# A two-stage kernel on one Trainium2 core: expert 0's last three blocks by seven half-size products, and a new instruction order for the first stage

## The chip, the cores and the metric

The program runs on one core of one Trainium2 chip. The metric is the device time of one execution in microseconds (us). Before the change three runs took 753.22, 753.16 and 752.12 us; the median is 753.16.

A core has five engines with queues of their own, each of which works in order: TensorE (PE; matmuls, with PEld for its weight loads), VectorE (DVE), ScalarE (ACT), GpSimd (POOL) and SyncE (SP). Matmul results land in PSUM, eight banks of 128 partitions x 2 KB; SBUF is the working memory. Transfers are issued by an engine's queue and run on 16 DMA engines.

## What is computed

Cross attention between tokens `x` and a small state, in both directions, makes a matrix of 4352 rows (8 batches of 512 + 32 rows) by 512 columns. It goes through a mixture of 8 experts, with routing weights from a Sinkhorn normalisation of 8 rounds.

```python
def _attn_ref(x, state):                      # x 8,8,512,64; state 8,8,32,64
    scores = scale * np.matmul(x, state.transpose(0, 1, 3, 2))
    a = np.exp(scores - scores.max(-1, keepdims=True))
    a /= a.sum(-1, keepdims=True) + 1e-09
    xread = np.matmul(a, state)
    scores2 = scale * np.matmul(state, x.transpose(0, 1, 3, 2))
    a2 = np.exp(scores2 - scores2.max(-1, keepdims=True))
    a2 /= a2.sum(-1, keepdims=True) + 1e-09
    sread = np.matmul(a2, x)
    return np.concatenate([xread, sread], axis=2)

def _moe_ref(x, w_gate, w1, w2):              # x 4352,512; w1 8,512,1024; w2 8,1024,512
    logits = x @ w_gate
    P = np.exp(logits - logits.max())
    for _ in range(8):
        P /= P.sum(1, keepdims=True) + 1e-09
        P /= P.sum(0, keepdims=True) + 1e-09
        P *= N / E
    for e in range(E):
        h = np.maximum(x @ w1[e], 0.0)
        out += P[:, e:e + 1] * (h @ w2[e])
    return out
```

## The kernel before

**Blocks.** The rows are cut into nine blocks: blocks 0 to 7 are the 512 tokens of a batch, block 8 holds the 256 state rows of all batches. Matmul operands are fp16, sums fp32. For blocks 0 to 7 the token rows are never formed: `aT` holds the attention weights, and the first layer uses V = state x w1 (L863 on: projections of 64x32 tiles, two halves `f` for each block), so a tile of 128 hidden units by 512 tokens is two matmuls (L897, L255). Block 8 uses `xsT` and four matmuls of 256 columns.

**Two parts.** The first part (to about 136 us) does attention, the whole of expert 0, Sinkhorn, and the first hidden block of expert 1. It is written as a list of operations `ops`, each with the engines that may do it, its predecessors and its buffers. `PLAN` (L18 to L50) is an order table: each step is the number of an operation and the letter of the engine. `issue` (L105) emits the operations in that order, so it sets the order of every engine's queue. The second part is the loop at L1042 over experts 1 to 7 and their blocks: the second layer of one block is interleaved with the first layer of the next.

**Attention.** Each batch has two units q of four heads; there are 16 units. For a unit: scores in PSUM (L605; the ring "pair" has one slot of two banks); side A transposes by VectorE (L628), maximum (L631), subtraction subA (L648, VectorE), exp (ScalarE), sum and reciprocal (L666, L667), normA (L670, VectorE or GpSimd), transpose back into `aT` (L674). Units 0 and 1 go another way: scores token by token (L684), maxT, subT (L691), and TensorE transposes (turnA L709). Side B takes the maximum (L640), exp (L652), a reciprocal (L659), normB (L662, on GpSimd in 12 units as a tensor_scalar), a transposing transfer on SP's queue (L742), and the matmuls of `read` (L758) that make `xsT`. GpSimd's queue issues the loads of `x_nat` (L468, four buffers) and of weights; SP's queue issues the transposing transfers of `x_nat` to `xT` (L591) from batch 2 on, in one line with those of L742.

**Expert 0.** For each block the hidden tiles go through PSUM to `hT` with a ReLU (L425 on ScalarE or L427 on VectorE). The second layer is dense: for each 128 tokens eight matmuls of 512 columns (L935), then one copy to `acc` (L419 or L421). After Sinkhorn `weigh` (L292) scales the rows of `acc` by expert 0's routing weight.

**Sinkhorn.** Part K: a maximum over the logits (L815), then eight rounds of `rownorm` (five VectorE instructions L829 to L833), a matmul with a matrix of ones (L846), and `colnorm` (three VectorE instructions). The routing weights `Pmat` are needed by the first accumulation of expert 1.

**Experts 1 to 7.** The second layer uses a form of 2x2 block multiplication with seven products in place of eight (`layer2`, L320): the 2x2 quarters are of tokens and hidden units on one side and of hidden units and output columns on the other. Sums of quarters of w2 are in `T` (L204, L965), sums of quarters of the hidden block in `sm` (L281 to L284). A product is eight matmuls of 256 columns into bank A, E or one of two banks B (`seeds`). A product's bank is added to `acc` with the routing weight (L348). Before expert 1's first products two matmuls with the identity (`seed`, L351) write the banks B once.

**End.** The last block's second layer writes its 256 rows in four transfers for each 128 rows, on two queues (L316 to L318).

Of the kernel before, what the change touches and what calls it, by code (L numbers as in the profile page):

```python
# [17 lines left out]
46V 62P 50H 51G 61A 71V 63P 60A 52G 64V 11G 72V 73A 80P 65V 12G 435P 401P 66A 81V 13H 79P 14G 82V 436A 88V  # L18
437A 404P 83A 67V 402A 137H 403A 89V 96H 97P 100P 84V 406A 68V 90A 98A 15G 85V 69P 86P 53G 405A 99V 87V 70A
103P 101A 102A 91V 409P 16H 92G 413P 104V 407P 410A 411P 105V 111A 438P 120P 414V 408A 419P 421P 106V 415P  # L20
112V 138S 121V 74V 439A 412A 422V 113V 417P 107A 54G 440A 75G 122V 432P 429P 123V 370V 420A 469P 128A 418A
416A 17G 108V 140P 124A 125V 423P 426P 471A 433P 114A 148V 93S 129V 430P 149V 172H 424P 76S 434A 115V 470A
109G 130V 139S 110V 126G 141V 131A 427P 18G 127V 142V 428V 431A 445P 143V 132V 94P 150A 95V 77P 425A 156P 116G
447P 151V 133V 78V 449P 446A 443P 441P 144A 455P 164V 152G 448A 117S 19H 450V 157V 444A 165V 173S 442A 451P
456A 166A 134S 20G 452A 453P 463P 158V 472P 207H 145V 175P 159V 183V 184V 457P 31G 146G 454A 176V 473A 160A
464P 185A 174S 460P 458P 461P 465A 147V 161V 21G 153S 177V 191P 47P 162G 474A 118P 167V 459A 154P 462A 178V
163V 135P 49A 168G 199V 22H 48V 179A 466P 136A 352P 475P 200V 192V 201A 193V 119V 467P 476A 194V 23G 195A 485P
202V 208S 210P 180V 169S 155A 218V 356P 353A 481P 357V 468A 487P 219V 24G 489P 181G 186V 211V 242H 486A 482A
477P 490V 488A 483P 479P 220A 170P 478A 503P 187G 480A 484V 171A 203G 196V 537P 209S 25H 212V 226P 197G 504A
505A 506P 213V 500P 182V 198V 26G 234V 221V 507A 222V 204S 188S 491P 27G 538A 227V 539A 501P 497P 502A 508A  # L30
492P 235V 243S 228V 244S 214A 229V 511P 215V 236A 523P 230A 498P 494P 216G 245P 495P 515P 512V 499A 277H 231V
524A 493A 517P 246V 253V 223S 496A 247V 521P 516A 237V 254V 519P 509P 522V 518A 248V 513P 232G 189P 520A 255A
205P 510V 224P 514V 540P 28H 278S 261P 249A 190V 269V 29G 225A 270V 262V 531P 534P 206V 238G 250V 532P 256V
358P 271A 535P 217V 541A 533A 233V 542A 312H 279S 263V 272V 536A 354P 280P 528P 543P 529P 525P 288V 289V 251G
555P 264V 281V 265A 282V 239S 257V 526P 359A 266V 544A 530V 556A 545P 355A 547P 549P 273G 553P 527A 546V 571P
313S 290A 548A 283V 605P 550A 554V 296P 267G 606V 304V 572A 305V 240P 573A 557P 284A 607A 558A 551P 297V 552A
568P 360P 258S 241V 285V 30G 291V 306A 559P 562P 574P 298V 252V 315P 299V 286V 569P 576A 268V 323V 563P 575A
274S 300A 560P 570A 292G 316V 361A 561A 581P 564A 307V 565P 362P 324V 317V 301V 325A 302G 566P 363V 582A 326V
579P 587P 583P 287V 314S 588V 591P 567A 580A 639P 608P 584A 592A 347H 303V 331P 577P 348G 641V 640A 610A 609A
339V 293S 589P 585P 275P 332V 259P 578A 327G 586A 260A 590A 294P 340V 308G 333V 341A 593P 309S 318V 319A 334V  # L40
295V 364P 594P 276V 328S 625P 619P 342V 595A 335A 365A 599P 320V 602P 343V 336V 600P 337V 603P 626A 321G 322V
329P 310P 350G 344S 601A 349G 311A 620V 345P 338V 346V 604V 366P 596P 330A 368P 369V 351G 597P 367A 371V 611P
372P 598A 695H 615P 617P 373V 612V 374P 375V 613P 614V 616A 623P 618A 621P 696H 711H 376A 705P 377V 642P 624A
622A 706A 707A 630P 643V 697V 708P 644A 378P 379V 631P 710A 627P 698V 380V 647P 632A 709A 636P 628P 381P 633P
699V 648V 637P 382V 634P 657P 629A 638A 383V 700V 653P 658A 655P 384P 651P 635A 701V 654A 725P 385V 723P 386V
702V 656A 726A 716P 652A 724A 717A 645P 659P 649P 714P 646A 650A 660A 387P 721P 715A 712P 727P 687P 722A 388V
728A 688A 667P 713A 664P 389V 390P 703V 665P 668P 391V 673P 674A 392V 661P 670P 669A 729V 393P 671P 394V 666A
662P 672A 677P 395V 718P 663A 678A 679P 675P 683P 719A 681P 720V 680A 676A 685P 396P 684A 682A 397V 686A 692P
704V 689P 693P 690P 730P 398V 694A 399P 733P 731V 691A 732A 735A 734A 400V
""".split()  # L50
ENGINES = {"P": "PE", "V": "DVE", "A": "ACT", "G": "POOL", "D": "DMA", "S": "SPQ", "H": "HOST"}
NT_ = 2
ETX = 0
POOLB = 1
X_PACE = 4.4
# [49 lines left out]
def issue(ops):  # L105
    for step in PLAN:
        op = ops[int(step[:-1])]
        assert all(d.end for d in op.after) and ENGINES[step[-1]] in op.on
        for slot in op.takes:
            slot.ring.taken.append(slot)  # L110
            slot.tile = slot.make()
        op.emit(ENGINES[step[-1]])
        op.end = True
    assert all(op.end for op in ops) and len(PLAN) == len(ops)
# [3 lines left out]
def kernel(  # L118
# [63 lines left out]
    outs = out.rearrange("(b s) d -> b s d", s=SB)[:, S:, :]  # L182
# [80 lines left out]
    def layer1(e, bi):  # L263
# [6 lines left out]
        for j in range(NJ):  # L270
            for i in range(2):
                fb = i * NJ + j
                hps = bank([128, S], FP32, "hps", "h")
# [25 lines left out]
    def layer2_last():  # L299
# [4 lines left out]
        nb = 128 // Ns  # L304
        for row in range(tn // 128):
# [10 lines left out]
            for i in range(nb):  # L316
                (nc.scalar if i % 2 else nc.sync).dma_start(
                    out=outs[row * nb + i], in_=acc[ds(i * Ns, Ns), k, :])  # L318

    def layer2(e, bi, n):  # L320
# [30 lines left out]
        def seed(i):  # L351
            bb = bank([128, 2, DH], FP32, "Bseed", "B%d" % i)
            nc.tensor.matmul(bb.rearrange("p c d -> p (c d)"), identh, aT[:, 0, 0], start=True, stop=True)
            seeds.append(bb)

        if not n:
            for k, eng in enumerate(("DVE", "ACT", "DVE", "POOL")):
                weigh(k, eng)
        product(A, h(0, 0), w2h[:, :NJ, :DH], True)
        if not n:  # L360
            seed(0)
        Bb = seeds[n % 2]
        nc.scalar.copy(out=Bb[:, :nk], in_=A[:, :nk])  # L363
        yield
        product(Eb, s(0), T[:, 0], True)
        if not n:
            seed(1)
# [199 lines left out]
    for b in range(B):  # L567
# [30 lines left out]
        for q in range(NQ):  # L598
# [62 lines left out]
            def normB(eng, E2=E2, rrec=rrec):  # L661
                engines[eng].tensor_scalar(out=E2.tile, in0=E2.tile, scalar1=rrec.tile, scalar2=None,  # L662
                                           op0=ALU.mult)
# [33 lines left out]
            else:  # L697
                m0 = op(r(2), {"DVE": (0.63, 0.72)}, flip, [o2], [eA], [ps])
                m1 = op(r(3), {"DVE": (0.59, 0.68)}, maxA, [m0], [mxA], [eA])
                s1 = op(r(4), {"DVE": (0.60, 0.80)}, subA, [m1], [], [eA, mxA])  # L700
# [22 lines left out]
            n2 = op(r(3), {"DVE": (0.10, 0.25)}, biasB, [m2], [nsB], [nmB])  # L723
# [5 lines left out]
            f2 = op(r(6), {"DVE": (0.16, 0.26)}, recB, [e2], [rrec], [rowsum])  # L729
            f2 = op(r(6), {"DVE": (0.35, 0.48), "POOL": (1.56, 1.70)} if POOLB else {"DVE": (0.35, 0.48)}, normB, [f2], [], [E2, rrec])  # L730

# [32 lines left out]
            def keepS(eng, b=b, q=q, su=su):  # L764
                copy(eng, xsT[:, ds(2 * q, 2), ds(b * Ns, Ns)], su.tile)
# [38 lines left out]
    def sk(on, emit, after, **how):  # L804
        return op(rank, on, lambda _: emit(), after, **how)
# [6 lines left out]
    op((30.0,), {"DVE": (0.2, 0.3)}, lambda _: nc.vector.memset(ones128, 1.0))  # L812
# [8 lines left out]
    c = sk({"PE": (0.18, 0.45)}, lambda: nc.tensor.matmul(gb.tile, ones128[0:1, :], sm_["gm"]), [c], takes=[gb])  # L821
# [4 lines left out]
    for it in range(8):  # L826
        def rownorm():
            rsum = tile_of("rsum", [128, NTB])
            nc.vector.reduce_sum(out=rsum, in_=Pmat, axis=AX_X)  # L829
            nc.vector.tensor_scalar(out=rsum, in0=rsum, scalar1=EPS, scalar2=None, op0=ALU.add)  # L830
            nc.vector.reciprocal(out=rsum, in_=rsum)
            nc.vector.tensor_mul(Pmat, Pmat, rsum.unsqueeze(2).broadcast_to((128, NTB, E)))
            nc.vector.reduce_sum(out=tile_of("cpart", [128, E]), in_=Pmat.transpose([0, 2, 1]), axis=AX_X)  # L833

        csb = psum([128, E], FP32, "csb_ps")

        def colnorm(csb=csb):
            crec = tile_of("crec", [128, E])
            nc.vector.tensor_scalar(out=crec, in0=csb.tile, scalar1=EPS, scalar2=None, op0=ALU.add)
            nc.vector.reciprocal(out=crec, in_=crec)  # L840
            nc.vector.scalar_tensor_tensor(out=Pmat, in0=crec.unsqueeze(1).broadcast_to((128, NTB, E)),
                                           scalar=float(N) / float(E), in1=Pmat,
                                           op0=ALU.mult, op1=ALU.mult)

        c = sk({"DVE": (2.10, 2.25)}, rownorm, [c])
        c = sk({"PE": (0.25, 0.60)}, lambda csb=csb: nc.tensor.matmul(csb.tile, ones128, sm_["cpart"]),  # L846
               [c], takes=[csb])
        c = sk({"DVE": (0.75, 0.90)}, colnorm, [c], uses=[csb])
# [193 lines left out]
    for i, (e, bi) in enumerate(work):  # L1042
# [11 lines left out]
        if i:  # L1054
            next(v, None)
# [54 lines left out]
```

## Time and profile before

| what | us |
|---|---|
| median of three runs | 753.16 |
| the profiled execution | 752.75 |
| its span, from first to last instruction | 751.0 |
| first matmul (waits for x_nat) | 6.86 |
| first reduction of Sinkhorn | 100.13 |
| last VectorE instruction of Sinkhorn ends | 136.09 |
| first product of expert 1 | 135.14 |
| last product ends, about | 747.0 |

Times within the profile are counted from the start of the span. Busy time of GpSimd is 70.8 us in all; 22272 packets with 20.97 MB are on its queue. The page's issues of transfers give the time from issue to landing:

```profile
w1h<-in_moe_w_dram POOLq DMA_DIRECT2D x16, 512.0 KB, 7.0
...
x_nat<-in_x_dram POOLq DMA_DIRECT2D x16, 256.0 KB, 5.6
...
xT<-x_nat SPq DMA_TRANSPOSE x12, 4.2
```

The columns are queue, kind, count, size and the median time to landing. An x_nat load is some six microseconds under way from GpSimd's queue, and its transposed copy four more from SP's.

A timeline line reads: start, duration, engine, line, operation, output and input tiles with their shapes, count, and in brackets how long the engine had been idle and what ended it. Neighbouring instructions of one engine overlap by some 0.07 us in the records.

### The profile page before, as it was taken

What the parts mean: (1) busy time and instruction counts of PE and PEld (TensorE: products, weight loads), DVE (VectorE), ACT (ScalarE), POOL (GpSimd) and SP (SyncE); (2) the same over time, 40 slices, a digit from 0 to 9 for tenths busy, and PEclk for the clock granted to TensorE, in tenths of its full rate; (3) what the DMA queues carried; (4) which work ended last, traced back from release to release, by engine and by line L of the source; (5) the groups of instructions that cost most, each with busy time, mean ns of one, the idle gap of its engine ahead of it and who ended that gap; (6) DMA issues with size and microseconds to landing.
All of it is one profiled execution on the core that took longest, in us unless ns stands there. A gap on an engine that the chain in (4) does not pass through costs nothing.

```text
span 751.0 us, 16151 instructions
## 1 busy us (share of the span) xinstructions
PE 736.0 (98%) x6517; PEld 502.2 (67%) x6517; DVE 617.0 (82%) x1529; ACT 517.7 (69%) x1014; POOL 70.8 (9%) x81
## 2 busy tenths in 40 slices
PE   5999999999999999999999999999999999999997
PEld 3444445666777777776776767776777767767776
DVE  5899989877888789788888788887897888887885
ACT  6876856799876766667666766667666676667662
POOL 4674410200010000100000000100001000000000
PEclk9899999999999999999999999999999999999999
DMA  9997560600033000700007000330007000002234
GB/s 179 140 134 131 82 99 1 109 6 1 1 61 53 2 1 2 113 1 2 1 2 112 2 1 1 58 57 1 1 2 112 2 1 2 1 31 94 103 113 141
DMA packets 51323, 36.71 MB, mean 49 GB/s; under 512 B 25392, under 2 KB 43824, under 8 KB 51248
## 3 DMA queue, kind: packets, MB, share of 16 engines
q0 software_dynamic: 22272, 20.97, 18.5%
q1 hardware_dynamic: 27744, 14.18, 7.6%
q8 instruction: 51, 0.84, 0.5%
q10 hardware_dynamic: 1232, 0.52, 0.3%
q14 instruction: 24, 0.20, 0.1%
HBM read 42.48 MB, written 8.91 MB: 68 GB/s over the span
## 4 chain that ended last, share of the span: by engine, by line
PE 92%; DVE 3%; DMA 1%; ACT 1%; POOL 1%; issue 0%; SPq 0%; POOLq 0%; DVEq 0%; ACTq 0%
PE hps L255 28%; PE Bseed L334 20%; PE A L334 14%; PE E L334 14%; PE yps L935 6%; PE hps L897 4%; PE v_ps L235 4%; DMA xT<-x_nat 1%; DMA x_nat<-in_x_dram 1%; PE y L312 0%; PE v_ps L870 0%; POOL a L670 0%; ACT Hm L275 0%; DVE acc L348 0%; POOL E L662 0%; PE su_ps L758 0%
## 5 line engine op out<-in xcount | busy, mean ns | idle before, releaser
L275 ACT ACTIVATE Hm<-hps 128x512 f16<-128x512 f32 (+1 forms) x496 | 265.8, 577 | 130.5 <-PE hps L255 128.1
L255 PE MATMUL hps<-aT,V 128*128 128x512 f16 x880 | 230.6, 379 | 0.0
L334 PEld LDWEIGHTS <-Hm 128*128 128x128 f16 x1888 | 181.6, 98 | 71.3 <-issue 15.9
L348 DVE SCALAR_TENSOR_TENSOR acc<-Bseed,Pmat,acc 128x256 f32<-128x256 f32 x354 | 155.0, 477 | 9.8 <-PE Bseed L334 6.9
L334 PEld LDWEIGHTS <-sm 128*128 128x128 f16 x1416 | 138.3, 98 | 34.5 <-issue 0.3
L334 PE MATMUL A<-w2h,Hm 128*128 128x256 f16 x944 | 123.7, 273 | 0.0
L334 PE MATMUL Bseed<-T,Hm 128*128 128x256 f16 x944 | 123.3, 273 | 0.0
L255 PEld LDWEIGHTS <-V 128*128 128x128 f16 x880 | 86.1, 98 | 50.8
L348 DVE SCALAR_TENSOR_TENSOR acc<-E,Pmat,acc 128x256 f32<-128x256 f32 x236 | 103.2, 476 | 13.8 <-PE E L334 13.5
L281 DVE TENSOR_TENSOR sm<-Hm 128x512 f16<-128x512 f16 (+1 forms) x122 | 50.1, 411 | 60.4 <-ACT Hm L275 60.2
L243 ACT CAST V<-v_ps 128x512 f16<-128x512 f32 x144 | 74.2, 612 | 0.0
L348 DVE SCALAR_TENSOR_TENSOR acc<-A,Pmat,acc 128x256 f32<-128x256 f32 x118 | 51.9, 479 | 17.9 <-PE A L334 17.6
L935 PE MATMUL yps<-w2h,hT 128*128 128x512 f16 x272 | 64.1, 379 | 0.1
L334 PE MATMUL E<-w2h,sm 128*128 128x256 f16 x472 | 61.7, 273 | 0.0
L334 PE MATMUL E<-T,sm 128*128 128x256 f16 x472 | 61.6, 273 | 0.0
L334 PE MATMUL Bseed<-T,sm 128*128 128x256 f16 x472 | 61.5, 272 | 0.0
L363 ACT COPY Bseed<-A 128x512 f32<-128x512 f32 (+1 forms) x62 | 34.1, 550 | 37.9 <-PE A L334 35.3
L282 DVE TENSOR_TENSOR Hm<-Hm 128x512 f16<-128x512 f16 (+1 forms) x122 | 50.3, 412 | 4.2
L284 DVE TENSOR_TENSOR sm<-Hm,sm 128x512 f16<-128x512 f16 (+1 forms) x122 | 50.2, 412 | 4.2
L283 DVE TENSOR_TENSOR sm<-sm,Hm 128x512 f16<-128x512 f16 (+1 forms) x122 | 49.4, 405 | 0.0
L194 POOL DMA_DIRECT2D w1h<-in_moe_w_dram x12 | 8.5, 714 | 396.9 <-PE hps L255 396.5
L935 PEld LDWEIGHTS <-hT 128*128 128x128 f16 x272 | 25.4, 99 | 28.9 <-issue 1.8
(127 smaller groups left out, 617.7 us busy)
## 6 DMA issues: line engine op xcount, KB each, us to landing
w1h<-in_moe_w_dram POOLq DMA_DIRECT2D x16, 512.0 KB, 7.0
w2h<-in_moe_w_dram POOLq DMA_DIRECT2D x16, 512.0 KB, 8.4
out_dram<-acc SPq DMA_DIRECT2D x32, 256.0 KB, 2.5
x_nat<-in_x_dram POOLq DMA_DIRECT2D x16, 256.0 KB, 5.6
st_st<-in_state_dram ACTq DMA_DIRECT2D x1, 256.0 KB, 4.9
st_st<-in_state_dram SPq DMA_DIRECT2D x1, 256.0 KB, 4.2
ETs<-E SPq DMA_TRANSPOSE x16, 4.3
out_dram<-acc SPq DMA_DIRECT2D x4, 64.0 KB, 1.8
```

What stands on the lines that cost most here:

```text
L235: nc.tensor.matmul(ps[q][ds(j * Ns, Ns), :], stT[ds(r, 64), bi, q, ds((j ^ q) * Ns, Ns)], w1h[ds(r, 64), 2 * q + j // 2, cols], tile_posit ...
L243: nc.scalar.copy(out=dst, in_=src)
L255: nc.tensor.matmul(out, lhs, rhs, start=(k == 0), stop=(k == len(terms) - 1))
L275: nc.scalar.activation(out=Hm[:, i, j, :tn], in_=hps[:, :tn], func=AF.Relu)
L281: nc.vector.tensor_add(s1, a21, a22)
L282: nc.vector.tensor_sub(a21, a11, a21)
L283: nc.vector.tensor_sub(s2, s1, a11)
L284: nc.vector.tensor_sub(s4, a12, s2)
L334: nc.tensor.matmul(dst[:, c], lhs(j, c), rhs[:, j], start=first and c == 0 and j == 0, stop=(j == NJ - 1), skip_group_check=True)
L348: nc.vector.scalar_tensor_tensor(out=dst, in0=src[:, c], scalar=p[:, k], in1=dst, op0=ALU.mult, op1=ALU.add)
L363: nc.scalar.copy(out=Bb[:, :nk], in_=A[:, :nk])
L935: nc.tensor.matmul(yps.tile, hT[fb].tile[:, ds(tk * 128, 128)], w2h[:, fb, :], start=(fb == 0), stop=(fb == NFB - 1))
```

## The change

It does six things. (1) Expert 0's blocks 6, 7 and 8 use seven products in the second layer: `strassen_ops` takes the place of the dense form, with sums of w2's quarters made by `sums_w_ops(0)` and of the hidden block's by `sums_h_ops`, each of which may stand on VectorE or GpSimd. The products are not weighted, so they are copied or added to `acc`. (2) The order table is new, and names more operations (833 in place of 736): the five and three VectorE instructions of a Sinkhorn round are operations of their own, so that others can stand between them. (3) A table `IDLE` puts dummy matmuls of 128 columns ahead of five operations. (4) normB on GpSimd is a product with a broadcast column in place of a tensor_scalar, and subA may stand on GpSimd. (5) The two seed matmuls go: the first hidden tile of block (1, 1) is computed in the first bank B, which writes it; the scalings of rows before expert 1's first adds are ordered anew. (6) The state rows are laid out so that 128 rows leave in one transfer for each group of columns.

The planner's cost figures beside the operations changed too; they are not used when the program is built.

```diff
 PLAN = """
 6G 0S 1S 2V 7H 44V 3A 33V 32A 34A 8G 56P 36P 35V 55H 37V 10H 45V 57A 42P 58V 9G 38P 40P 43A 59P 4S 39A 41V 5V
...
+IDLE = {56: 50, 63: 3, 80: 3, 462: 8, 69: 22}
+SB0 = (6, 7, 8)
...
+        idle(op.takes[0].tile if op.takes else None, IDLE.get(int(step[:-1]), 0))
         op.emit(ENGINES[step[-1]])
...
-    outs = out.rearrange("(b s) d -> b s d", s=SB)[:, S:, :]
+    nb = 128 // Ns
+    outs = out.rearrange("(g b s) d -> g s b d", b=nb, s=SB)[:, S:, :, :]
...
-                hps = bank([128, S], FP32, "hps", "h")
+                if lent is None:
+                    hps = bank([128, S], FP32, "hps", "h")
+                else:
+                    hps, lent = lent, None
...
-            for i in range(nb):
-                (nc.scalar if i % 2 else nc.sync).dma_start(
-                    out=outs[row * nb + i], in_=acc[ds(i * Ns, Ns), k, :])
+                (nc.scalar if c + 1 < parts else nc.sync).dma_start(
+                    out=outs[row, :, :, cols], in_=acc[:, k, cols])
...
-        def seed(i):
-            bb = bank([128, 2, DH], FP32, "Bseed", "B%d" % i)
-            nc.tensor.matmul(bb.rearrange("p c d -> p (c d)"), identh, aT[:, 0, 0], start=True, stop=True)
-            seeds.append(bb)
-
         if not n:
-            for k, eng in enumerate(("DVE", "ACT", "DVE", "POOL")):
+            for k, eng in ((2, "DVE"), (3, "POOL"), (0, "DVE")):
                 weigh(k, eng)
         product(A, h(0, 0), w2h[:, :NJ, :DH], True)
+        Bb = seeds[n % 2]
         if not n:
-            seed(0)
-        Bb = seeds[n % 2]
+            yield
         nc.scalar.copy(out=Bb[:, :nk], in_=A[:, :nk])
+        if not n:
+            weigh(1, "ACT")
...
-                engines[eng].tensor_scalar(out=E2.tile, in0=E2.tile, scalar1=rrec.tile, scalar2=None,
-                                           op0=ALU.mult)
+                if eng == "POOL":
+                    nc.gpsimd.tensor_mul(E2.tile, E2.tile, rrec.tile.broadcast_to((128, S)))
+                else:
+                    nc.vector.tensor_scalar(out=E2.tile, in0=E2.tile, scalar1=rrec.tile, scalar2=None, op0=ALU.mult)
...
-                s1 = op(r(4), {"DVE": (0.60, 0.80)}, subA, [m1], [], [eA, mxA])
+                s1 = op(r(4), {"DVE": (0.60, 0.80), "POOL": (1.05, 1.20)}, subA, [m1], [], [eA, mxA])
...
-                copy(eng, xsT[:, ds(2 * q, 2), ds(b * Ns, Ns)], su.tile)
+                copy(eng, xsT.rearrange("p c (g n b) -> p c g n b", g=B // nb, b=nb)[:, ds(2 * q, 2), b // nb, :, b % nb], su.tile)
...
+    def sums_w_ops(e):
...
+        for g in range(2):
+            tg = []
+            for i in range(4):
+                def sub(eng, i=i, g=g):
+                    p, q = quarters(e, tsum[e])[i]
+                    jj = ds(g * (NJ // 2), NJ // 2)
+                    engines[eng].tensor_sub(tsum[e][:, i, jj], p[:, jj], q[:, jj])
...
+    def sums_h_ops(bi, rank, kept, Hm, sm, goal=None):
...
+            def t1(eng, parts=parts):
+                a11, a21, a12, a22, (s1, s2, s4) = parts()
+                engines[eng].tensor_add(s1, a21, a22)
...
+            on = {"DVE": (0.15 + 0.29 * f, 0.25 + 0.29 * f), "POOL": (0.1 + 0.95 * f, 0.25 + 0.95 * f)}
...
+    def strassen_ops(bi, deps, held, Tr):
...
+            def seed(_):
+                nc.tensor.matmul(pair.tile[:, 0], identh, aT[:, 0, 0], start=True, stop=True, skip_group_check=True)
...
+        p1 = product(A, h(0, 0), lambda: w2(0, 0), True, a11 + [ready], [Ab])
+        c1 = op(rank, {"ACT": (0.50, 0.66), "DVE": (0.62, 0.74)}, lambda eng: copy(eng, Bb()[:, :nk], A()[:, :nk]),
+                [p1] + st_last, [], [pair, Ab])
+        p2 = product(Eb, s(0), lambda: T(0), True, s1 + Tr[0] + [ready] + st_last)
+        e11 = put(Eb, 1, 1, [p2])
+        p3 = product(Bb, s(1), lambda: T(1), False, s2 + Tr[1] + [c1])
+        e01 = put(Bb, 0, 1, [p3])
+        p4 = product(A, h(1, 0), lambda: w2(1, 0), False, a12 + [c1])
+        put(A, 0, 0, [p4])
+        p5 = product(Bb, h(0, 1), lambda: T(2), False, s3 + Tr[2] + [e01])
+        x11 = put(Bb, 1, 1, [p5, e11], True)
+        p6 = product(Eb, s(2), lambda: w2(1, 1), False, s4 + [e11])
+        x01 = put(Eb, 0, 1, [p6, e01], True)
+        p7 = product(Bb, h(1, 1), lambda: T(3), False, a12 + s3 + Tr[3] + [x11])
+        y = put(Bb, 1, 0, [p7])
...
+        if bi in SB0:
+            h_ready = strassen_ops(bi, deps, held, Tr0)
+            continue
...
+    def idle(t, n):
...
+        for _ in range(n):
+            if t.dtype == FP16:
+                nc.tensor.transpose(t, identh, identh)
+            else:
+                nc.tensor.matmul(t, identh, identh, start=True, stop=True, skip_group_check=True)
...
+        if not i:
+            seeds += [bank([128, 2, DH], FP32, "Bseed", "B%d" % k) for k in range(2)]
         l2 = layer2(e, bi, i)
-        l1 = layer1(*work[i + 1]) if i + 1 < len(work) and work[i + 1] not in hid else iter(())
+        l1 = iter(())
+        if i + 1 < len(work) and work[i + 1] not in hid:
+            l1 = layer1(*work[i + 1], None if i else seeds[0].rearrange("p c d -> p (c d)"))
+        if not i:
+            next(l2)
+            next(l1)
```

In the new order GpSimd does 12 normB, 12 normA, 12 subA, 7 of the 16 half-sums of w2 (5 for expert 0, 2 for expert 1) and 13 sums of quarters of H; VectorE keeps 2 subA, does 8 of the 80 ReLUs (it did 16) and 9 half-sums of w2. Sinkhorn's first reduction stands behind 42 hidden groups and 40 dense half-groups of TensorE's order, where it stood behind 50 and 48.

## Prediction

> **What bounds the kernel now.** I read the page first: busy shares and the chain that ended last.
>
> ```profile
> PE 736.0 (98%) x6517; PEld 502.2 (67%) x6517; DVE 617.0 (82%) x1529; ACT 517.7 (69%) x1014; POOL 70.8 (9%) x81
> ...
> PE 92%; DVE 3%; DMA 1%; ACT 1%; POOL 1%; issue 0%; SPq 0%; POOLq 0%; DVEq 0%; ACTq 0%
> ```
>
> TensorE carries the chain. The change, however, is almost wholly in the first 136 us (attention, expert 0, Sinkhorn), so next come three windows of that stage. The columns are span, then busy us (and count) of PE, weight loads, DVE, ACT, POOL, then granted clock, DMA share, GB/s.
>
> ```profile
> 0.00:23.00 23.00, 14.00 (x145) 8.20 (x146) 14.12 (x32) 14.46 (x28) 9.84 (x17) 0.85 1.18 179
> 23.00:100.00 77.00, 75.47 (x866) 35.95 (x859) 71.02 (x160) 58.99 (x134) 41.57 (x39) 1.00 0.81 117
> 100.00:136.00 36.00, 35.73 (x227) 18.27 (x225) 31.93 (x89) 22.62 (x47) 0.00 (x0) 1.00 0.20 34
> ```
>
> To 23 us TensorE is little used and its clock is not all granted (0.85). From 23 to 100 us VectorE is at 92% beside a full-looking TensorE; from 100 us GpSimd is empty. Matmuls are pipelined, so "busy" hides small waits; the timeline of TensorE shows them.
>
> ```profile
> 18.86 3.57 PE L897 MATMUL hps<-aT,V 128*128 128x512 f16 x8
> ...
> 22.98 1.90 PE L897 MATMUL hps<-aT,V 128*128 128x512 f16 x8
> ...
> 52.82 0.30 PE L605 MATMUL psB<-xT,stT 64*32 64x256 f16 x8 [0.90 <-DMA xT<-x_nat]
> ```
>
> The same eight matmuls take 3.57 us cold and 1.90 us warm. At 52.82 the scores wait for a transposing transfer. From starts of consecutive matmuls in the timeline I get the streaming price of each form: 0.216 us for 512 columns, 0.109 for 256, 0.025 for a gate product; for the small tiled groups, the usual time from one group's start to the next.
>
> TensorE's floor from 22.98 us to the first product of expert 1 (135.14 us): 272 yps x 0.216 = 58.8; 136 hps x 0.216 = 29.4; 32 x 0.109 = 3.5; 15 groups of V projections x 0.23 = 3.4; 12 of scores x 0.22 = 2.7; 16 of reads x 0.3 = 4.8; gates 2.4; Sinkhorn's small products 2. Sum 107.0 of 112.2: **5.2 us are waits**. Nothing else in that stage can be won except by doing less on TensorE.
>
> **1. Dummy matmuls and the clock.** 50 dummies of 128 columns stand before the first transposes. Those transposes have a pitch of 107 ns (eight from 6.86 us); 50 x 0.107 = 5.35 us. The identity they read is ready at 1.29 us, so they end by 6.7, inside the wait for x_nat that ends at 6.86: they cost nothing. If x_nat came at once they would cost 5.35. 22 more stand before the first turnA, under VectorE's normA; uncovered they cost 1.2 to 2.4 us. With the clock up, the eight hps from 18.86 us take 1.9 instead of 3.57: -1.7. They do not start earlier: the 32 earlier transposes shrink by up to 1.7 us, but the new order puts one more xT copy (0.35 us net) ahead of keepA on VectorE, and three more PSUM copies (0.6 us each) ahead of the second expA on ScalarE. I take **-1.7**; bounds 0 and -3.4.
>
> The Trainium skill ("TensorE: Matmul & The Clock Gate", section Part 1) says that the gate opens after a busy window of about 3.4 us and closes after an idle one. By it the dummies warm the array before x_nat lands; but the gate may shut again before 18.86 us, when TensorE waits on the attention chain, and the -1.7 would be 0. The halved pitch at 18.86 us, after matmuls at 10 to 15 us, agrees with such a closing.
>
> **2. Seven products.** Blocks 6, 7, 8 lose 32 + 32 + 16 = 80 matmuls of 0.216 us (17.3) and get 56 + 56 + 28 = 140 of 0.109 (15.3) and one seed (0.2): **-1.8** on TensorE, which counts only where TensorE sets the end; bound 0.
>
> **3. Work moved, and the waits.** Before Sinkhorn's first reduction (L814, at 100.13 us) VectorE loses 12 of 14 subA (0.60 us from start to start, two of them held to 1.17), six ReLUs and one PSUM copy (0.61 each) and gets two xT copies (0.35): -11.8 us. With VectorE's idle time as it was Sinkhorn starts at 88.3; were TensorE never waiting after 19 us, at about 82 (the new order has 62.5 us of TensorE work at those prices between the first hps and there). I take 85.
>
> After it VectorE gets 11 half-sums of H and one more of T (0.42 each), six PSUM copies and adds (0.62: rows L427 and L691 have 0.68, less the 0.07 by which neighbours overlap), and loses two ReLUs: +7.6. Sinkhorn's stretch was 100.13 to 136.09 = 36.0, so 43.6, and the end is 128.6. TensorE has 43 us from there (38 hidden tiles, 8 dense and 21 seven-product groups, 8 projections) against 34 before: 128. So the front ends near 128 to 129 by both engines, against 135.14. Taken on TensorE alone the same is -1.7 - 1.8 and a part of the 5.2 us of waits. I choose **-2.0** for that part; bounds -5.2 and, as a loss, the lock below.
>
> GpSimd gets 12 subA, 7 half-T and 13 half-sums, none of which the trace has there. Nearest rows: its TENSOR_TENSOR of 128x512, 1.05 us (L670), and its TENSOR_SCALAR, 1.57 (L662) to 1.85 (L296). I take 1.05, as the operation is that of L670, also for normB, which becomes a TENSOR_TENSOR (1.57 to 1.05). Before Sinkhorn that is 36 x 1.05 + 16 loads x 0.8 = 50.6 us of some 66; at 1.85 it would be 79 and GpSimd the bound. GpSimd issues x_nat loads in order behind these, and the scores wait for the transposes of those loads (52.82 us above): late there is late for all attention.
>
> **4. Behind the front.** Two seed matmuls between expert 1's first products go (136.03 and 137.28 us, about 0.22 each): **-0.45**. Three row scalings instead of four precede the first adds, no gain counted. At the end:
>
> ```profile
> 746.06 2.30 SPq L317 DMA_DIRECT2D out_dram<-acc  x4
> 746.06 2.33 ACTq L317 DMA_DIRECT2D out_dram<-acc  x4
> ```
>
> Four issues of 0.58 us on each queue, two of them after the last add (747.5); now one remains there, of 128 KB. That saves 0.58 and may land later: rows give 1.8 us for 64 KB and 2.5 for 256. I take **-0.3**; bounds -0.6 and +0.2.
>
> **Sum:** -1.7 - 1.8 - 2.0 - 0.45 - 0.3 = -6.25 on the span of 751.0. The profiled execution took 752.75 with 1.75 around the span, 0.41 below the median 753.16. So 746.5 against its own time, **746.9, say 747.0**, against the median.
>
> **Rivals.** *The port between VectorE and GpSimd (slower).* Two pairs from the timeline:
>
> ```profile
> 41.54 1.04 POOL L670 TENSOR_TENSOR a<-eA,rA 128x512 f16<-128x512 f32 x1 [1.59 <-DVE rA L667]
> ...
> 70.50 1.56 POOL L662 TENSOR_SCALAR E<-E,rrec 128x512 f16<-128x512 f16 x1
> ```
> ```profile
> 41.96 1.17 DVE L648 TENSOR_TENSOR eA<-eA,mxA 128x512 f32<-128x512 f32 x1
> ...
> 71.09 0.68 DVE L648 TENSOR_TENSOR eA<-eA,mxA 128x512 f32<-128x512 f32 x1
> ```
>
> Beside GpSimd's TENSOR_TENSOR the subtraction ends only 0.55 us after GpSimd does (1.17 long); beside its TENSOR_SCALAR, which reads SBUF too, it runs undisturbed (0.68). In Sinkhorn's stretch, where GpSimd was empty, the new order has about 17 us of GpSimd TENSOR_TENSORs among VectorE's 44 two-input instructions (16 of Sinkhorn, 9 of T, 11 and 8 of sums). Put blindly, 44 x 17/45 = 17 of them would start inside one, each losing half to all of 0.85 us: 7 to 14, and 128.6 becomes 136 to 143. From 6.5 us lost on, the front is no faster. Against it: the sums are interleaved with reductions, and the subA that met the lock leave VectorE. Price at 9.5 us: 137.1 + 0.95 of lead lost, **about 755**.
>
> The Trainium skill ("SBUF — State Buffer", section Who interferes with whom) gives an exclusive lock for any GpSimd read beside a two-input VectorE instruction. By it normB's new form would cost no more blocking than its old one; the 0.68 us at 71.09 disagrees, and the measurement decides.
>
> *Smaller gain.* The clock falls back before 18.86 us, and waits only move (DMA, PSUM slots): -1.8 - 0.45 - 0.3: **750.6**. For it: 92% on VectorE with in-order queues, and GpSimd's subA now in each attention unit's chain. *All waits vanish:* -3.4 - 1.8 - 5.2 - 0.75 = -11.2: **742.0**; against it, VectorE's 43.6 us. *Not done as said:* excluded, the changed program's order has the 140 products.
>
> **How the numbers follow.** My forecast (gain 4 to 9 us, 744 to 749) 0.52; smaller gain 0.20; all waits gone 0.10; within 0.2% (1.5 us, what this kernel's measurement can tell) 0.06; lock 0.12. Faster 0.82, same 0.06, slower 0.12. The range 741.5 to 752.5 leaves out most of the lock and little else.
>
> **What would show it.** Right: hps from about 19 us at 0.216 pitch; Sinkhorn's first reduction at 82 to 88; expert 1's first product at 127 to 131; the stretch from there to the last add shorter by about 0.45. Wrong: granted clock 0.5 around 19 us; L296-like or TENSOR_TENSOR rows on GpSimd well above 1.05; VectorE products of Sinkhorn above 0.44 us; TensorE waiting for VectorE ahead of expert 1's first adds; scores waiting for xT longer than 0.9 us.

## The result, and the profile after

The changed kernel takes 758.44 us (median of 6 runs, 757.74 to 760.84) where the kernel before took 752.84 in the same comparison (6 runs): a ratio of 1.0079, 95% interval 1.0065 to 1.0093. It is slower by about 6 us; 747.0 was forecast. The profiled execution has a span of 756.4 us where before had 751.0. One execution of e7 below took 1542.67 us, twice the others; it is left out of e7's ratio, and the only trace of e7 is of it.

The first lines of the page, its busy shares and the chain that ended last:

```profile
PE 739.1 (98%) x6662; PEld 512.6 (68%) x6662; DVE 615.1 (81%) x1529; ACT 522.7 (69%) x1025; POOL 95.4 (13%) x113
...
PE 88%; DVE 5%; DMA 4%; ACT 2%; issue 1%; POOL 0%; SPq 0%; POOLq 0%; ACTq 0%; DVEq 0%
```

TensorE has fallen from 92% to 88% of that chain, VectorE and the transfers have gained. The windows of the first stage, with the columns of those before (span, busy PE, weight loads, DVE, ACT, POOL, granted clock, DMA share, GB/s):

```profile
0.00:18.00 18.00, 14.37 (x279) 12.09 (x280) 11.19 (x29) 12.34 (x26) 7.52 (x15) 1.00 1.17 179
18.00:90.00 72.00, 67.25 (x751) 31.65 (x745) 62.75 (x150) 54.98 (x125) 49.39 (x53) 1.00 0.91 128
90.00:105.00 15.00, 13.11 (x82) 5.36 (x80) 11.81 (x27) 10.53 (x21) 6.54 (x7) 0.89 0.60 94
105.00:141.00 36.00, 33.21 (x267) 23.12 (x266) 28.52 (x75) 23.04 (x51) 12.57 (x14) 1.00 0.10 16
```

The clock is all there up to 90 us, as the dummies were to bring. But TensorE, busy for 35.73 of 36 us after Sinkhorn's start in the kernel before, is now busy for 13.11 of 15 and 33.21 of 36, and the clock is down to 0.89 for a while.

| us, in the profiled executions | before | after |
|---|---|---|
| first hidden tile of expert 0 starts | 18.86 | 17.96 |
| its eight matmuls, to the start of what follows | 4.12 | 2.07 |
| Sinkhorn's first reduction | 100.13 | 89.20 |
| first product of expert 1 | 135.14 | 140.99 |
| between these two | 35.0 | 51.8 |
| TensorE's work between these two, by the forecast's prices | 34.1 | 43.0 |
| first product of expert 1 to the end of the span | 615.86 | 615.4 |

The lines behind the rows of Sinkhorn and of expert 1, before, then after (VectorE, TensorE):

```profile
100.13 0.44 DVE L814 TENSOR_REDUCE lmx<-logits 128x1 f32<-128x272 f32 x1
```
```profile
135.14 1.05 PE L334 MATMUL A<-w2h,Hm 128*128 128x256 f16 x8
```
```profile
89.20 0.44 DVE L822 TENSOR_REDUCE lmx<-logits 128x1 f32<-128x272 f32 x1
```
```profile
140.99 1.03 PE L344 MATMUL A<-w2h,Hm 128*128 128x256 f16 x8 [0.46 <-ACT acc L424]
```

All of the loss lies ahead of expert 1's first product (+5.85); behind it 0.45 is gained. If from a stretch of time I subtract the work that TensorE does in it, by the same prices, what is left is an estimate of the time that TensorE loses there. From the end of the first hidden tiles (22.98 before, 20.03 after) to 40 us it loses 0.3 us before and 3.4 after; from there to Sinkhorn's first reduction 3.3 and 3.5; in the stretch behind it 0.9 and 8.8. So the lead of 3 us from the warm start was gone by 40 us. Sinkhorn starts 11 us earlier only because some 11 us less of TensorE's work stand ahead of it, of which 9 stand behind it now; and that stretch loses 8.8 us where it lost under 1.

At the start and at the end, in the timeline:

```profile
17.96 1.90 PE L918 MATMUL hps<-aT,V 128*128 128x512 f16 x8
...
23.34 0.30 PE L610 MATMUL psB<-xT,stT 64*32 64x256 f16 x8 [0.88 <-DMA xT<-x_nat]
```
```profile
751.51 2.05 SPq L327 DMA_DIRECT2D out_dram<-acc  x2
752.12 0.65 ACTq L327 DMA_DIRECT2D out_dram<-acc  x1
```

The eight matmuls take 1.90 us as forecast, and the scores of the third batch wait for a transposing transfer behind them. In the last microseconds there are now single transfers; the last add ends 3.44 us before the end of the span, where it was 3.5.

The lost time in Sinkhorn's stretch has two kinds of place. First, what waits of TensorE the trace lists from Sinkhorn's first reduction to expert 1: waiting tile and line, what it waited for, us in total, times, the longest. Before, then after:

```profile
PE csb_ps L846 <- DVE cpart L833: 0.3, 1, 0.3
```
```profile
PE csb_ps L866 <- DVE cpart L850: 2.3, 2, 1.9
PE BE L1055 <- ACT acc L424: 1.1, 2, 0.7
PE BE L1055 <- DVE acc L1066: 0.5, 1, 0.5
PE A L344 <- ACT acc L424: 0.5, 1, 0.5
```

The matmul with ones (csb) waits for VectorE, and the products of expert 0 (tile BE, two banks) wait for the copies and adds that empty the banks. Second, the longest of these waits, on three engines:

```profile
92.70 2.04 DVE L841 TENSOR_SCALAR rsum<-rsum 128x34 f32<-128x34 f32 x1
```
```profile
92.42 2.27 POOL L954 TENSOR_TENSOR T<-w2h,T 128x512 f16<-128x512 f16 x2
```
```profile
96.43 0.36 PE L866 MATMUL csb_ps<-cpart,ones 128*128 128x8 f32 x2 [1.86 <-DVE cpart L850]
...
97.51 3.54 PE L918 MATMUL hps<-aT,V 128*128 128x512 f16 x8
```

An addition of 128x34 numbers, usually 0.18 us, takes 2.04: it ends when the second of two half-sums on GpSimd ends (94.69). TensorE waits 1.86 us for what follows from it, and behind the wait its clock is granted at half from 97.59 to 101.0, so eight matmuls take 3.54 us. It is no accident of one execution: the two experiments with the same order there (e6, e8) have the same row at 2.04 and 2.32 us, waits of 1.9 and 2.1 us, and 3.4 us of half clock behind them. From 17 to 143 us such stretched rows of VectorE have some 5.5 us in excess of their usual time (1 in the kernel before), 4.2 of them in the stretch.

### The profile page after: what moved, and what is told of

The parts are those of the page before. It is cut to its first block, busy times and chain, and to the rows that moved or that the text cites. A ratio compares the mean times of both kernels' runs of the same rounds, so it can differ in the third digit from the quotient of the medians.

```text
span 756.4 us, 16484 instructions
## 1 busy us (share of the span) xinstructions
PE 739.1 (98%) x6662; PEld 512.6 (68%) x6662; DVE 615.1 (81%) x1529; ACT 522.7 (69%) x1025; POOL 95.4 (13%) x113
## 4 chain that ended last, share of the span: by engine, by line
PE 88%; DVE 5%; DMA 4%; ACT 2%; issue 1%; POOL 0%; SPq 0%; POOLq 0%; ACTq 0%; DVEq 0%
PE hps L264 28%; PE Bseed L344 20%; PE A L344 14%; PE E L344 13%; PE v_ps L244 4%; PE hps L918 3%; PE yps L1128 2%; DMA xT<-x_nat 2%; PE BE L1055 1%; DMA x_nat<-in_x_dram 1%; ACT Hm L287 0%; PE y L323 0%; DVE nmB L645 0%; PE A L1055 0%; DVE acc L358 0%
## 5 line engine op out<-in xcount | busy, mean ns | idle before, releaser
L264 PE MATMUL hps<-aT,V 128*128 128x512 f16 x878 | 230.1, 379 | 0.0
L368 ACT COPY Bseed<-A 128x512 f32<-128x512 f32 (+1 forms) x62 | 34.1, 549 | 37.9 <-PE A L344 35.3
L1128 PE MATMUL yps<-w2h,hT 128*128 128x512 f16 x192 | 44.8, 379 | 0.0
L918 PE MATMUL hps<-aT,V 128*128 128x512 f16 x144 | 36.8, 393 | 0.7 <-DVE xsT L426 0.7
```

The source lines that it names most:

```text
L264: nc.tensor.matmul(out, lhs, rhs, start=(k == 0), stop=(k == len(terms) - 1))
L918: nc.tensor.matmul(ps.tile[:, :tn], lhs, rhs, start=(k == 0), stop=(k == len(terms) - 1))
L1128: nc.tensor.matmul(yps.tile, hT[fb].tile[:, ds(tk * 128, 128)], w2h[:, fb, :], start=(fb == 0), stop=(fb == NFB - 1))
```

## The experiments

Times are medians beside runs of the kernel before on the same chip (752.1 to 753.1 us); a ratio is to those, with its 95% interval. "Stretch" is the time from Sinkhorn's first reduction to expert 1's first product. Stretches and lines are from one profiled execution of each kernel; those of e5 and e12 took 2.3 and 2.2 us more than their medians.

**e1: the two half-sums off GpSimd.** In the changed kernel's order table:

```diff
-452G 453V ... 456G ... 454V ... 458V
+453V ... 452V 454V ... 456V 458V
```


> The changed kernel with two of GpSimd's five half-sums of expert 0's w2 (those that follow its load of w1h, at 92.42 us in the changed kernel) on VectorE, later in its order. Port theory: the first eps addition of Sinkhorn (L841) takes 0.18 us in place of 2.04, the wait of the ones-matmul behind it (1.86 us) and the half clock from 97.59 to 101.0 us (1.7 us) go, 0.8 us of VectorE work comes: first product of expert 1 at about 137.3 in place of 141.0, about 754.8. Rival, the new order's waits only move to the next wait on TensorE's queue: 757.5 or more.

756.63 us, 1.0056 (1.0038 to 1.0074), between the two forecasts. L841 takes 0.18 us, the csb wait and the half clock behind it are gone, the stretch is 48.5 us for 51.8. The hold with what follows from it is thus worth 3.3 us in the stretch. The median shows 1.8; in the profiled execution the first hidden tile starts 1.8 us later (19.74), with the clock at half from 14.04 to 17.45 us.

**e2: blocks 6 to 8 dense again, in the new order.** Products are replaced by dense groups in the same places; the sums are not issued.

> The changed kernel and its order, with the second layer of blocks 6, 7, 8 dense again from the same hidden tile (64 + 16 matmuls of 512 columns); the half-sums of expert 0's w2 and of the hidden blocks issue nothing. Theory that the sums are to blame (port, VectorE's load, clock): Sinkhorn's stretch loses some 4 us of port waits, 6 us of VectorE work and the half clock, TensorE gets 1.8 us: 752 to 754. Rival, the order of the first 90 us and its late transfers are to blame: 757 or more.

757.65 us, 1.0056 (1.0036 to 1.0076). No row of VectorE is held in the stretch, yet it lasts 48.9 us. Without products and sums the stretch is thus 2.9 us shorter, no more than e1 gained by moving two half-sums; the products' 1.8 us can't be seen in the time. The time is the rival's, but most of the loss is still in the stretch and not in the first 90 us. The groups still went into the two banks of BE, with waits of 1.2 us there: the hint for e5.

**e3: the dummies alone, in the kernel before.**

```diff
+IDLE = {56: 50, 63: 3, 80: 3, 404: 8, 69: 22}
```


> The kernel before with the dummy matmuls alone (50, 3, 3, 8, 22). The term of the prediction, -1.7: 751.1 beside 752.8, with the eight hps at 18.9 us in 1.9 us. Rival, TensorE gets ahead and then waits for transfers that come no earlier: 752.3 to 753.3, with longer waits of the scores for xT.

754.04 us, 1.0026 (1.001 to 1.0041). The eight matmuls take 2.27 us for 4.12, but start at 20.48 us, so they end 0.2 us earlier than before (22.75 for 22.98). The clock had been at half again from 15.4 to 18.7 us, and the 22 dummies ahead of turnA (17.64 to 19.42) ran while its input was ready (15.93). The warm start is given back there; the waits of the scores for transfers behind it, the rival's mechanism, are no longer than before (1.0 us in all for 1.3).

**e4: eight half-sums of w2 on GpSimd, in the kernel before.**

> The kernel before with expert 1's eight half-sums of w2 on GpSimd (they stand on VectorE before). If VectorE gets the port only when GpSimd pauses: the eight run in one piece of some 9 us, one of Sinkhorn's eps additions (L830) or products (L832, L841) in it takes several us, up to 8, in place of 0.18 or 0.44, and the time is 755 to 760. If it gets the port after one GpSimd instruction: no row over 1.3 us, at most 3 us lost against 2.8 us less on VectorE: 752.3 to 753.5.

753.7 us, 1.0016 (1.0005 to 1.0026). Rows of VectorE are stretched by 0.52 us at most, 2.2 in all. The time is up by about 1.2 us. Half-sums on GpSimd are thus not dear everywhere; in the changed kernel two in a row fell on a bad place.

**e5: one tile for each bank.** The two banks BE of the seven products are one tile of the program. In e1's trace (timeline of TensorE, ScalarE, VectorE):

```profile
111.94 0.29 PE L866 MATMUL csb_ps<-cpart,ones 128*128 128x8 f32 x2
112.94 1.03 PE L1055 MATMUL BE<-T,Hm 128*128 128x256 f16 x8 [0.71 <-ACT acc L424]
```
```profile
111.32 0.58 ACT L424 COPY acc<-BE 128x512 f32<-128x512 f32 x1 [1.10 <-PE BE L1055]
...
112.29 0.59 ACT L424 COPY acc<-BE 128x512 f32<-128x512 f32 x1
```
```profile
114.95 0.69 DVE L1066 TENSOR_TENSOR acc<-BE,acc 128x512 f32<-128x512 f32 x1 [2.28 <-PE BE L1055]
```

Product 5 writes the first bank, which the copy at 111.32 empties by 111.90. It starts at 112.94, with the end of the second copy (112.88), which reads the other bank. The add at 114.95 needs product 5 alone (done at 113.97) and starts when product 6, in the other bank, is done (114.85).

```diff
-            pair = Slot(rings["pair"], lambda: bank([128, 2, 512], FP32, "BE", "pair"))
+            def make_pair():
+                pair_ctx.close()
+                for tag in ("SB", "SE"):
+                    pools[tag] = pctx.enter_context(
+                        tc.tile_pool(name="psum_" + tag, bufs=1, space=bass.MemoryType.PSUM))
+                return [bank([128, 2, DH], FP32, tag, tag) for tag in ("SB", "SE")]
+            pair = Slot(rings["pair"], make_pair)
...
-        Bb = lambda: pair.tile[:, 0].rearrange("p (c d) -> p c d", c=2)
-        Eb = lambda: pair.tile[:, 1].rearrange("p (c d) -> p c d", c=2)
+        Bb = lambda: pair.tile[0]
+        Eb = lambda: pair.tile[1]
```


> The kernel e1_two_subs, whose two-bank PSUM tile of the seven products (named BE) is made two tiles of one bank each; order and arithmetic are the same. Theory: a product into one bank now waits for the copy out of the OTHER bank, since both are one tile; in e1's trace product 5 of block 6 starts at 112.94 us, when the copy out of the other bank ends (112.88), though its own bank was free at 111.90; the add at 114.95 starts when the product into the other bank ends; 128.22 and 136.14 us are the same. Four such places cost TensorE 0.9, 0.7, 0.6 and 0.5 us and delay VectorE by 1.1 once. So from Sinkhorn's first reduction to the first product of expert 1 I expect 45.5 to 47 us in place of 48.5, and 754.0 to 755.3 us as the median (e1 756.6). Rival: VectorE and the matmuls with ones bind the stretch, and the waits only move: 48 us or more, and 756 us or more.

753.44 us, 1.0009 (0.9995 to 1.0024); the stretch is 45.4 us. The same place, and the only wait of TensorE left in the stretch's list:

```profile
113.84 0.29 PE L867 MATMUL csb_ps<-cpart,ones 128*128 128x8 f32 x2
113.99 1.03 PE L1063 MATMUL SB<-T,Hm 128*128 128x256 f16 x8
```
```profile
115.13 0.69 DVE L1074 TENSOR_TENSOR acc<-SB,acc 128x512 f32<-128x512 f32 x1 [0.56 <-PE SB L1063]
```
```profile
PE A L345 <- ACT acc L425: 0.5, 1, 0.5
```

Product 5 now starts 0.15 us after the matmul with ones in place of 1.00, and the add 1.14 us after its product's start in place of 2.01. No order and no arithmetic was changed, so the waits were false ones, between banks that have nothing to do with each other: 3.1 us of the stretch and 3.2 of the median. e9 to e12 keep the two tiles and the order from Sinkhorn on, and their four traces have the same stretch of 45.4 us.

**e6: no dummies, in the changed kernel.** `IDLE = {}`.

> The changed kernel with an empty table of dummy matmuls, all else the same. Theory (what the dummies gain is given back before Sinkhorn, because the transfers of x set the pace of attention): the first hidden tiles run cold again (3.5 us for eight) and start within 1.5 us of 18 to 20 us, Sinkhorn's first reduction stays within 1 us of 89 to 91.5, and the time is 757.5 to 759.5. Rival (the dummies are worth the 1.7 us of the forecast): Sinkhorn's first reduction 1.5 to 3 us later and 760 us or more. If they harm, 757 or less.

760.4 us, 1.0093 (1.0075 to 1.0112), with Sinkhorn's first reduction at 92.06 us. These are the rival's numbers, though the interval overlaps the changed kernel's: in the new order the dummies gain between nothing and some 3 us; in the old one (e3) they don't.

**e7: parts 5 and 6 alone, in the kernel before.**

> The kernel before with parts 5 and 6 of the change alone: no seed matmuls, first hidden tile of block (1, 1) in the first bank B, the scalings of rows in their new order, the state rows leaving in one transfer for each group of columns. Theory: -0.45 for the seeds and 0 to -0.3 for the end, as from the first product of expert 1 to the end in the two traces (615.86 and 615.4): 752.1 to 752.5 against 752.8. Rival: the lent bank or the three scalings delay expert 1's first products, and nothing is gained: 752.7 to 753.3.

753.4 us, 1.0007 (0.9994 to 1.0019). The 0.45 us that the two traces show from expert 1's first product to the end is not to be seen as a time, and the interval holds both the theory's gain and the rival's nothing.

**e8: the subtractions of attention on VectorE again.** Twelve steps of the order table, `123G` to `318G`, get the letter V.

> The changed kernel with the 12 subA of attention on VectorE again, at their places in the order, all else the same. Theory (attention is paced by the transfers of x and by waits between engines, not by VectorE's sum of work): Sinkhorn's first reduction at 89 to 92.5 us and 757 to 760 us. Rival (VectorE sets the pace, as the forecast took it): 12 x 0.6 = 7.2 us more on VectorE, Sinkhorn's first reduction at 94.5 us or later and 762 us or more.

766.53 us, 1.0181 (1.0162 to 1.0199); Sinkhorn's first reduction at 98.9 us. The theory falls: 7.2 us more on VectorE come out as 9.7 at Sinkhorn and 8 in the time. Part of the 9.7 may be the clock: e8's trace has two stretches of 3.4 us at half ahead of Sinkhorn (from 46.5 and 63.5 us), the change's has none. In the new order, the move of subA to GpSimd is needed, not idle.

**e9: without the 22 dummies ahead of the first turnA** (on e5). Timeline of e5, VectorE then TensorE; then TensorE of e9:

```profile
14.39 0.68 DVE L678 TENSOR_TENSOR a<-eA,rA 128x512 f16<-128x512 f32 x1
```
```profile
15.54 2.53 PE L1200 MATMUL aT_ps<-identh 128*128 128x128 f16 x22
17.86 0.63 PE L717 MATMUL aT_ps<-identh,a 128*128 128x128 f16 x4
```
```profile
15.22 0.61 PE L717 MATMUL aT_ps<-identh,a 128*128 128x128 f16 x4
```


> The kernel e5_split without the 22 dummy matmuls ahead of the first turnA (the other 64 stay). Theory: those 22 keep TensorE from work that is ready. VectorE ends the normA that turnA needs at 14.97 us in the trace of the change and at 15.07 in that of e5; turnA starts at 16.05 and, with the clock granted at half in 14 to 17.5 us, at 17.86. Without them turnA should start at 15.1 to 15.4, the first hidden tile at 17.3 to 18.5 in place of 20.43, and if this lasts to the end the time is 751 to 752.6 (e5 753.4). Rival (the transfers of x set the pace, as the scores of the third batch do not start before 23 us): the start is earlier but Sinkhorn's first reduction stays within 1 us of e5's 93.2, and the time is 753 to 754.

What turnA reads is ready at 15.07 us; TensorE is busy until 17.86, from 15.54 on with dummies, as its clock was granted at half from 12.7 to 19.6 us. Without them turnA starts at 15.22 and the first hidden tile at 17.99 in place of 20.43; Sinkhorn starts at 91.3 in place of 93.2. The time, 752.4 us, 1.0006 (0.9986 to 1.0027), can't be told from e5's, so theory and rival aren't told apart.

**e10 and e11: loads of x further apart** (on e9). `24G` behind `23G` and `27G` behind `229G`; or `26G` and `27G` behind `229G`. Three loads are issued at once; the second line is the time to landing of the transfers x_nat to xT from 50 to 62 us (shortest, median, longest). First e5, then e9, where the loads stand as in e5:

```profile
52.08 2.29 POOL L474 DMA_DIRECT2D x_nat<-in_x_dram  x3
```
```profile
DMA to landing us min/median/max: 3.3/3.3/7.3
```
```profile
52.32 2.29 POOL L474 DMA_DIRECT2D x_nat<-in_x_dram  x3
```
```profile
DMA to landing us min/median/max: 4.3/5.2/5.5
```


> The kernel e9_no22 with two of GpSimd's loads of x_nat moved in its queue: the second load of batch 5 goes from the place behind block 8's subA (52.1 us in e5) to behind the first load of batch 5 (about 45.5), the second load of batch 6 from 53.6 to behind unit 9's subA (about 57.7). Theory: at 52.08 us three loads of 256 KB are issued at once, beside them the transposing transfer to xT lands after 7.3 us (3.3 median), TensorE waits 3.06 us for it at 56.23, and its clock is granted at half for 3.4 us after that. With the loads apart the wait is 1 us or less, the clock stays, and the time is 1.5 to 3.5 us under e9. Rival (the earlier load only moves the collision to the transfers of batch 4, or VectorE, which sets the pace, hides the wait): within 0.7 us of e9.

> The kernel e9_no22 with both loads of batch 6 behind unit 9's subA (about 57.7 us) and the second load of batch 5 at its place (52.1). Theory as for e10_loads: one load instead of three beside the transfer to xT, a wait of 1 us or less at 56 us, 1 to 3 us under e9; if the transposing transfer of batch 5's second half now waits, the wait moves to the scores of unit 11 at about 63 us. Rival: within 0.7 us of e9.

e10: 752.7 us, 0.9996 (0.9984 to 1.0008). e11: 754.45 us, 1.0027 (1.0015 to 1.0039). The wait at 56 us that both were to remove (3.06 us above, 2.7 in the list of waits) is not in every trace with three loads at once: from 56 to 62 us the change, e1, e2 and e5 list 1.3 to 2.7 us of waits for transfers to xT, e6 and e9 none. e9, from which both start, has the three loads at 52.32 and no transfer there over 5.5 us. So against e9 neither tests the theory, and three loads at once don't by themselves cause the wait. The waits for transfers differ from trace to trace: the longest of TensorE is 2.3 us in e10 (up to 46.38), 2.4 in e9 (up to 47.54), 1.4 in e11. The time of e10 is as the rival has it; why e11 is some 2 us slower was not found.

**e12: eight copies out of PSUM from VectorE to ScalarE** (on e10): steps 504, 514, 540, 570, 608, 610, 600 and 631 get the letter A.

> The kernel e10_loads with eight copies out of PSUM ahead of Sinkhorn (six ReLUs of expert 0's hidden tiles, two copies of V) on ScalarE in place of VectorE, at their places in the order. That takes 8 x 0.61 = 4.9 us from VectorE, which e8_sub_dve showed to set the pace there when 7.2 us were added, and puts 8 x 0.5 = 4.0 us on ScalarE, which had some 17 us free in 18 to 90 us. Theory (VectorE's sum of work still sets the pace): Sinkhorn's first reduction 2.5 to 5 us earlier than e10's 90.3, the time 749 to 751. Rival (with the subtractions gone from it, the pace is set by the chain of transfers to xT and the waits between the queues): Sinkhorn's first reduction within 1.5 us of 90.3, the time 752 to 753.5.

754.8 us, 1.0038 (1.0021 to 1.0055); Sinkhorn's first reduction at 93.8 us, later by 3.5, which neither theory had. VectorE's longest waits from 18 to 90 us in e10, then in e12:

```profile
DVE nmB L646 <- PE psB L611: 4.7, 4, 1.5
```
```profile
DVE nmB L646 <- PE psB L611: 8.1, 7, 2.7
```

In this trace VectorE waits 3.4 us longer for scores, which wait for transfers of x, and 2.8 us longer for ScalarE (0.2 to 3.0), which got the copies. TensorE's clock was at half in it from 25.3 to 28.7 and from 49.3 to 52.6 us, behind waits of 2.3 and 2.0 us for transfers, while e10's was full; by the prices above that is an estimated 1.7 us of matmuls each, together as much as the 3.5. So relieving VectorE alone gains nothing, but what the eight copies cost is not shown by this one pair. With e8 this says that VectorE's sum of work is at the limit there; whether it alone sets the pace, or which link of the chain (transfer to xT, scores, VectorE, transfer of E, read, next load) does, was not settled. The waits differ from one execution to the next by a microsecond or two.

No version tried beats the kernel before: e5, e7, e9 and e10 can't be told from it.

## Why the prediction was wrong

The step that failed is term 3, work moved and the waits. It set the end of the first stage at 128.6 us: Sinkhorn's first reduction at 85 and 43.6 us behind it. It came at 89.2 and 51.8: 12.4 us too late, in two parts. (The 43.6 ran to VectorE's last instruction of Sinkhorn, TensorE's 43 to expert 1's first product; the first now ends at 142.06, the second starts at 140.99.) In the sum this is the -2.0: TensorE's waits behind the first hidden tiles were to shrink by two from 5.2 us; by the account above its lost time there grew from some 4.5 to 15.7.

*Sinkhorn's first reduction at 85 (+4.2).* VectorE's own sum with its idle time as it was gave 88.3. I went halfway to the 82 that TensorE would need without waits (64.2 us of work counted in the trace, not 62.5, so nearer 83), and nothing in the profile paid for that half: the page had shown VectorE at 92% and scores waiting for xT. 89.2 is near VectorE's own sum, and e8 shows that its work counts there. What else holds this part was not settled (e9 to e12).

*The stretch at 43.6 (+8.2).* I took the sums of two engines and assumed that they overlap. In the kernel before they did, with 0.3 us of listed waits; the new order puts products, copies, adds and the matmuls with ones of both engines in alternation, and each hand-over can wait. e1 and e5 price the two that mattered: the held addition, 3.3 us (51.8 to 48.5), and the false waits between the two banks, 3.1 us (48.5 to 45.4). The 1.8 us left were not taken apart; e5's trace lists waits of VectorE of up to 0.6 us, and rows of it stretched by 3.0 us in all. Where to look could have been seen beforehand: that BE is one tile of two banks stands in the changed code, and the new order says which GpSimd instructions lie beside Sinkhorn.

*The lock* was a rival with 0.12. e1 bears its mechanism out, but its size came from the wrong rows: I counted 44 two-input instructions of VectorE and priced them alike, at 7 to 14 us; the stretched rows there have 4.2. The dear one has one input (L841 of the changed kernel, the addition), and what cost the most was the csb wait and the half clock behind it. The Trainium skill ("SBUF — State Buffer", section Who interferes with whom) names tensor_scalar among the operations that can take both ports when their operands meet its conditions, which the forecast left out. It also says that the one that comes second is blocked for the whole of the other's instruction; at 92.70 VectorE was held until a second instruction of GpSimd had ended, and there the measurement decides.

*Term 1, the clock (-1.7).* The eight matmuls won 2.05 us from start to start, and started 0.9 us earlier, which the forecast excluded; so the size was right, but not that it reaches the end: the lead was gone by 40 us, e3 gains nothing, and e6 leaves room for some gain in the new order alone. That the dummies cost nothing held for the first 50; the 22 ahead of turnA kept ready work waiting by 1.1 us (after) to 2.3 (e5, 15.54 to 17.86). The clock fell back to half between 12.6 and 19.6 us in seven of the nine other kernels with dummies (e1: 14.04 to 17.45 us), though not in e8, e12 and the change. That agrees with what the forecast took from the Trainium skill ("TensorE: Matmul & The Clock Gate", section Part 1), that the gate closes again after an idle window, but the time ahead of it was not empty: in e1 TensorE issued 96 small matmuls from 10.67 to 14.0 us, with waits of 0.7 us between them.

*Term 2, seven products (-1.8).* As TensorE's work yes; in the time it can't be seen (e2). *Term 4:* -0.45 between expert 1 and the end as forecast, -0.06 of it in the last transfers where -0.3 was taken; e7 can't tell it from nothing. GpSimd's rows in attention were as taken (1.03 to 1.07 us, one of 1.36); its sums of 128x512 took 1.12 to 1.27 us where 1.05 was taken.

## What to carry to other kernels

When work is moved between in-order queues, the two sums of busy time are a lower bound: walk through the new order hand-over by hand-over, above all where a serial chain on one engine (Sinkhorn) meets an accumulator that another must empty. Give each independently used PSUM bank a tile of its own, since waits may go by the tile. Put dummy work only where nothing real can become ready behind it. A lead won at the start may last only as far as the next transfers, as it did here. And before an experiment is aimed at one wait, look whether a second trace has it.

## What the hardware showed that I had not expected

- VectorE's 0.18 us addition was held for 2.04 us, across the rest of one GpSimd instruction and the whole of the next; elsewhere (e4) a row lost at most 0.52 us.
- One wait of TensorE of 1.9 us in otherwise dense work was followed by 3.4 us of half clock (97.59 to 101.0), which cost about as much again. It isn't a rule: e10 has a wait of 2.3 us (up to 46.38) with the clock full behind it.
- Transfers from x_nat to xT landed after 3.1 to 7.6 us (18 to 90 us, e5 and e9). One took 7.3 beside three loads of 256 KB in e5; in e9, beside the same three, the longest took 5.5.
